# The second MLP layer of a fused attention and mixer kernel in two groups of 1024 rows instead of four of 512

## The chip, the cores and the metric

The kernel runs on one core of a Trainium2 chip. Its engines work beside each other, each through a list of instructions in a fixed order: TensorE (PE, matmuls; PEld its weight loads), VectorE (DVE), ScalarE (ACT), GpSimd (POOL) and SyncE (SP, which here only issues DMAs). They wait for each other through semaphores. The metric is the device time of one execution in microseconds.

## The reference

```python
g = _sigmoid((x * gate_w).sum(-1, keepdims=True))
a = _A_ref(x, A_wqkv, A_wo)                # attention: 2048 rows, 32 heads of 16
b = _B_ref(x, B_w1, B_w2, B_w3, B_w4)
return g * a + (1 - g) * b
# _A_ref
scores = jnp.einsum("bhqd,bhkd->bhqk", q, k) * (Dh ** -0.5)
p = _softmax(scores, axis=-1)
o = jnp.einsum("bhqk,bhkd->bhqd", p, v)
# _B_ref: x is 2048 x 512, w1 and w2 512 x 512, w3 512 x 1792, w4 1792 x 512
h = _gelu(_layernorm(x, axis=-1) @ w1)
...   # four quarters of h's columns, shifted by 1, -1, 2, -2 rows, joined to hs
x1 = x + hs @ w2
h2 = _gelu(_layernorm(x1, axis=-1) @ w3) @ w4
return x1 + h2
```

Both halves take the same x, in bfloat16.

## The kernel before

Attention is cut into 32 units. A unit is one chunk c of 512 query rows with four heads (`units`, numbered 0 to 31), and has 64 blocks of 128 keys by 512 queries: 16 key tiles for each of four heads, 2048 blocks in all. TensorE computes a block's scores into a bank of PSUM. Then the exponential is taken in one of two ways:

- On ScalarE: one ACTIVATE (in `expo`, the tile `pt`) for all blocks of a step, two blocks (1024 columns) or three (1536). A step's scores lie in the tile `stage`. There are two of these, used in turn: the scores of step k are put in place after ScalarE has read step k-2 (`score_ready`).
- On VectorE and GpSimd: a "whole" block is read from PSUM (the tile `dsc`) by a TENSOR_SCALAR that turns scores into bits of an approximate exponential (`dump`). Four such blocks of a key tile fill one room of 128x4x512 int16. Three more instructions over all of the room (`shifted`, 128x2048) give further terms, the last of them on GpSimd in part. A chain thus is four blocks; its terms go to TensorE as five times four products (`produce`). A step that has one whole block beside it has two blocks for ScalarE, a step without one has three.

The rooms are seven tiles `quad`, two in `more` and, as they come free, the chunks of `xT`; they stand in the queue `room`. A new chain starts only with enough of them (`wants_whole`).

Beside the attention runs the job list `mlp()`: the first MLP layer, then the second (512 to 1792 and back to 512). For the second, the code before goes over four chunks c of 512 rows. In each, the normed rows come transposed into `xnT`; 8 of 14 column tiles of h2 are computed into the bank for general use (`ps_y`) and copied by VectorE to `g2T` (`before_gelu`). Then `gelu_all` waits until ScalarE has its turn: ACT_TABLE_LOAD for gelu, two ACTIVATEs of 128x2048 in place, two of 128x1536 straight from `stage` tiles with the 6 tiles that are left, ACT_TABLE_LOAD for exp, and a tiny ACTIVATE (`small`). No exponentials run on ScalarE in that stretch. After it `w4_tile` multiplies by w4. The same is done once for the first layer (`hT`).

At a unit's end its sums are copied from PSUM to `accsb` (L1171), a chain of DMAs brings the reciprocals of the denominators as `bcs`, GpSimd scales (`oT`, L1201), and `out_tile` (`ps_o`) projects and mixes. The last unit is cut in three ranges of rows to shorten the end (`finish_range`); there j is one of four row tiles, and j = 0 goes through ScalarE and GpSimd (L1306, L1309), the others through VectorE (L1299).

The order of all instructions is fixed when the program is written: a planner in the kernel goes step by step through estimated times of each engine and picks what to issue next. Its rules and costs are numbers in the code: `USUAL` and `RULES` (by unit) say when whole blocks are taken, among them `WIDE`, how many whole blocks a step may have, and `MAXD`, how many key tiles a unit may give to chains; others are `VLIM`, `LASTNEED`, `LOOK`, `SPARE`. `VK` says among how many key tiles chains may be chosen.

Of the kernel before, what the change touches and what calls it, by code (L numbers as in the profile page):

```python
# [32 lines left out]
def kernel(  # L33
# [21 lines left out]
    VK = 7  # L55
# [118 lines left out]
    VLIM = 2.0  # L174
    LASTNEED = 40
# [3 lines left out]
    LOOK = 0.1  # L179
    BACK = 0.6  # L180
    RUN = 1.5
    SPARE = 1
    HOLD = (0.15, 0.5)
    MARGIN = 0.3
    CREDIT = 0.5
    LATER = 0.55
    GELU, WTWO = 1.0, 1.6
# [5 lines left out]
    SLACK = 0.25  # L193
# [206 lines left out]
    def norm_T(n, c, res):  # L400
        yield all_at(*[("xn", n, 4 * c + j) for j in range(4)])
        xnT = xtpool.tile([P, KT, CH], BF16, tag="xnT", name="xnT")
# [59 lines left out]
    def w4_tile(g2T, w4, c, t):  # L462
        yield all_at("w4", ("g", c))
        ps = gen("ps_4")
        j = t % 4
        for m in range(FT):
            bmm(ps[:], lhsT=g2T[:, m, j * P:(j + 1) * P], rhs=w4[:, m, :],
                start=(m == 0), stop=(m == FT - 1))
            if m < FT - 1:
                yield MM  # L470

        def fn(end):
            nc.vector.tensor_tensor(out=x_sb[t][:], in0=x_sb[t][:], in1=ps[:], op=ALU.add)
            at["mix", t] = end

        evac(0.69, fn)
        yield MM

    def mlp():
# [28 lines left out]
        for c in range(NC_):  # L508
            if c < NC_ - 1:
                norm(1, c + 1)  # L510
            g2T = pools["g"].tile([P, FT, CH], BF16, tag="g", name="g2T")
            for m in range(APART):
                yield from before_gelu(w3, m, res[0], g2T[:, m, :], ("z", c, m), all_at(("xnT", 1, c, KT - 1)))
            yield from gelu_all(("g", c), [g2T[:, m:m + 4, :] for m in range(0, APART, 4)],
                                all_at(*[("z", c, m) for m in range(APART)]), w3, res[0],
                                [(range(m, m + 3), g2T[:, m:m + 3, :]) for m in range(APART, FT, 3)])
            if c < NC_ - 1:
                res = []
                yield from norm_T(1, c + 1, res)
            for t in range(4 * c, 4 * c + 4):  # L520
                yield from w4_tile(g2T, w4, c, t)
# [508 lines left out]
    def exp_option():  # L1030
# [6 lines left out]
        if k in turn:  # L1037
            return turn[k][2]() if turn[k][1] else t
# [9 lines left out]
    def expo_gelu(start, k):  # L1048
        key, parts, _, _, _, ms, dst, ending = turn[k]
        if parts:  # L1050
            start += LOAD
        for part in parts:
            nc.scalar.activation(out=part, in_=part, func=ACT.Gelu_apprx_tanh)  # L1053
            start += 0.1 + part.free_size() / 1200
# [4 lines left out]
        if ending:  # L1059
            at[key] = done_exp[k]  # L1060
            nc.scalar.activation(out=small[:], in_=mhalf[:, 0:1], func=ACT.Exp)
# [176 lines left out]
    def finish_range(r, ready):  # L1238
# [41 lines left out]
        def scale(end):  # L1280
# [3 lines left out]
            for j in range(a, b):  # L1284
# [3 lines left out]
                queue["pe"].append((2 - 3 * r, 2 * MM, lambda begin, j=j: out(j), fits))  # L1288
# [238 lines left out]
```

## Time and profile before

| | |
|---|---|
| median of 3 runs | 776.76 us (775.57 to 777.45) |
| the profiled execution: its own time | 777.28 us |
| its span, first to last instruction | 775.5 us |
| mean granted TensorE clock | 0.996 of full speed |
| busy: PE, DVE, ACT, POOL | 749.0, 718.0, 757.7, 254.3 us |
| chain that ended last | ACT 51%, PE 29%, issue 16%, DVE 2% |

A row of the view of groups gives line, engine, operation, tiles and shapes, the number of instructions, then their busy time together in us and the mean duration of one in ns, then the engine's idle time before them and who ended it. Consecutive ACTIVATEs overlap in the record, so that the mean duration is more than the time from one start to the next. In the timeline a row has start, length, engine, line, operation and the number of merged instructions (the form shown is that of the first), and in brackets the idle time before it.

### The profile page before, as it was taken

How to read it: one execution, taken by the hardware profiler on the slowest of the kernel's cores; microseconds unless marked ns; L12 is line 12 of the kernel's file. 1: busy time of each engine (PE TensorE's matmuls, PEld its weight loads, DVE VectorE, ACT ScalarE, POOL GpSimd, SP SyncE). 2: the span in 40 equal slices, each digit the busy share in tenths (PEclk: the TensorE clock that was granted, in tenths of full speed). 3: DMA queues.
4: the chain of work that ended last, by engine and by line, in shares of the span. 5: the costliest groups of instructions: out<-in, count | busy, mean ns of one | idle time of the engine just before them, and what ended most of it. 6: DMA issues, size and time to landing. Idle time of an engine off the chain costs nothing.

```text
span 775.5 us, 24000 instructions
## 1 busy us (share of the span) xinstructions
PE 749.0 (97%) x10166; PEld 245.6 (32%) x10166; DVE 718.0 (93%) x1234; ACT 757.7 (98%) x731; POOL 254.3 (33%) x190
## 2 busy tenths in 40 slices
PE   8999999999999999899999999999999999999997
PEld 4334323333333232232223223322332232332233
DVE  5798999999999999899999999999999989999993
ACT  6999999999999999899999999999999999999995
POOL 3221433442313414234442333123323412443420
PEclk9999999999999999999999999999999999999999
DMA  8600012111130005002000013000040000000010
GB/s 209 192 20 17 13 50 64 31 34 42 19 36 19 19 15 127 20 16 47 20 12 27 19 33 44 18 8 19 19 53 21 16 21 25 21 23 19 20 40 28
DMA packets 52307, 29.05 MB, mean 37 GB/s; under 512 B 36712, under 2 KB 47720, under 8 KB 52200
## 3 DMA queue, kind: packets, MB, share of 16 engines
q1 hardware_dynamic: 51240, 27.00, 15.1%
q8 instruction: 79, 1.29, 0.7%
q10 hardware_dynamic: 960, 0.52, 0.2%
q14 instruction: 28, 0.23, 0.1%
HBM read 17.17 MB, written 2.35 MB: 25 GB/s over the span
## 4 chain that ended last, share of the span: by engine, by line
ACT 51%; PE 29%; issue 16%; DVE 2%; DMA 1%; POOL 0%; POOLq 0%; ACTq 0%; DVEq 0%; SPq 0%
ACT pt L1076 47%; PE acc L1089 11%; PE stage L754 9%; PE ps L271 4%; PE ps_y L271 2%; ACT g2T L1053 1%; PE ps_o L271 1%; ACT g2T L1056 1%; ACT hT L1053 1%; DMA bcs<-rec_d 1%; ACT L1053 1%; PE warm L1330 0%; DVE quad L959 0%; DMA rec_d<-rec 0%; DVE quad L1000 0%
## 5 line engine op out<-in xcount | busy, mean ns | idle before, releaser
L1076 ACT ACTIVATE pt<-stage 128x1024 bf16<-128x1024 f32 (+1 forms) x687 | 707.7, 1207 | 4.1 <-PE stage L754 2.6
L754 PE MATMUL stage<-qT,kT 32*128 32x512 bf16 (+1 forms) x1597 | 271.7, 380 | 16.7 <-ACT pt L1076 12.4
L959 DVE TENSOR_SCALAR quad<-dsc 128x512 int16<-128x512 f32 x342 | 227.6, 683 | 13.2 <-PE dsc L754 10.9
L998 POOL TENSOR_SCALAR quad<-quad 128x2048 int16<-128x2048 int16 x71 | 134.9, 1901 | 261.9 <-DVE quad L1000 145.9
L754 PE MATMUL dsc<-qT,kT 32*128 32x512 bf16 x475 | 182.6, 384 | 0.0
L754 PEld LDWEIGHTS <-kT 32*128 32x128 bf16 x2072 | 81.9, 91 | 284.0 <-issue 250.3
L1000 DVE TENSOR_SCALAR quad<-quad 128x2048 int16<-128x2048 int16 x212 | 146.8, 705 | 2.3 <-PE acc L1089 1.9
L1089 PE MATMUL acc<-pt,vp 128*17 128x512 bf16 (+2 forms) x1572 | 147.4, 379 | 1.4 <-DVE accsb L1171 0.7
L1089 PE MATMUL acc<-quad,vp 128*17 128x512 bf16 x1696 | 145.4, 382 | 0.0
L1089 PEld LDWEIGHTS <-vp 128*17 128x17 bf16 (+1 forms) x4072 | 82.7, 89 | 131.1 <-issue 95.5
L271 PE MATMUL ps<-w,g2T 128*32 128x512 bf16 x896 | 70.5, 382 | 0.0
L1201 POOL TENSOR_TENSOR oT<-accsb,bcs 128x512 bf16<-128x512 f32 x29 | 37.1, 1278 | 66.1 <-DVE quad L1000 48.8
L271 PE MATMUL ps_y<-xnT,w 128*32 128x512 bf16 x704 | 56.2, 387 | 1.0 <-DVE accsb L1171 0.8
L959 DVE TENSOR_SCALAR more<-dsc 128x512 int16<-128x512 f32 x77 | 51.2, 681 | 1.8 <-PE dsc L754 1.6
L998 POOL TENSOR_SCALAR more<-more 128x2048 int16<-128x2048 int16 x17 | 32.3, 1900 | 61.2 <-DVE more L1000 31.6
L998 POOL TENSOR_SCALAR xT<-xT 128x2048 int16<-128x2048 int16 x13 | 25.0, 1924 | 69.8 <-DVE quad L1000 31.0
L1089 PE MATMUL acc<-more,vp 128*17 128x512 bf16 x424 | 40.4, 380 | 0.0
L959 DVE TENSOR_SCALAR xT<-dsc 128x512 int16<-128x512 f32 x56 | 37.3, 681 | 2.6 <-PE dsc L754 2.2
L271 PEld LDWEIGHTS <-w 128*32 128x32 bf16 x1152 | 28.0, 96 | 34.3 <-issue 17.2
L1089 PE MATMUL acc<-xT,vp 128*17 128x512 bf16 x380 | 36.0, 383 | 0.0
L271 PE MATMUL acc<-wq,zero 128*32 128x512 bf16 x324 | 29.8, 383 | 0.0
L271 PEld LDWEIGHTS <-g2T 128*32 128x32 bf16 x896 | 19.3, 95 | 22.1 <-issue 14.3
(117 smaller groups left out, 598.4 us busy)
## 6 DMA issues: line engine op xcount, KB each, us to landing
bcs<-rec_d SPq DMA_DIRECT2D x31, 256.0 KB
w<-in_B_w_dram SPq DMA_DIRECT2D x2, 1792.0 KB
out_dram<-ot SPq DMA_DIRECT2D x15, 128.0 KB
x_sb<-in_A_x_dram SPq DMA_DIRECT2D x14, 128.0 KB
oT<-oT SPq DMA_DIRECT2D x112, 16.0 KB
w<-in_B_w_dram SPq DMA_DIRECT2D x2, 512.0 KB
wkv<-in_A_wqkv_dram SPq DMA_DIRECT2D x1, 512.0 KB
wo_all<-in_A_wo_dram SPq DMA_DIRECT2D x8, 64.0 KB
```

The source lines that it names most:

```text
L271: nc.tensor.matmul(out[j:j + 32, :], lhsT=lhsT[:, j:j + 32], rhs=rhs, tile_position=(0, j), **kwargs)
L754: nc.tensor.matmul(out, lhsT=kT[G][32 * j:32 * j + 32, cc, o:o + P], rhs=qTs[(c, G)][32 * j:32 * j + 32, a, lo:hi], start=True, stop=True, ...
L959: nc.vector.tensor_scalar(out=bits[:, r:r + wide, :], in0=dsc.rearrange("p (a c) -> p a c", c=CH), scalar1=SHIFT, scalar2=LOWEST, op0=ALU. ...
L998: behind(nc.gpsimd.tensor_scalar(out=tiles[to], in0=tiles[base], scalar1=1.0, scalar2=shift, op0=ALU.mult, op1=ALU.add))
L1000: fast["ins"] = nc.vector.tensor_scalar(out=tiles[to], in0=tiles[base], scalar1=shift, scalar2=None, op0=ALU.add)
L1053: nc.scalar.activation(out=part, in_=part, func=ACT.Gelu_apprx_tanh)
L1056: nc.scalar.activation(out=dst, in_=stages.pop(k)[:, 0:len(ms) * CH].rearrange("p (a c) -> p a c", c=CH), func=ACT.Gelu_apprx_tanh)
L1076: nc.scalar.activation(out=pt[:, 0:w], in_=stages.pop(k)[:, 0:w], func=ACT.Exp, scale=LN2 / 128.0)
L1089: nc.tensor.matmul(accs[n][32 * j:32 * j + M, lo:hi], lhsT=lhsT, rhs=p, start=(kt == 0), stop=(kt == NT - 1), skip_group_check=True, tile_ ...
L1201: behind(nc.gpsimd.tensor_tensor(out=oT, in0=tiles["accsb"][:], in1=tiles["bcs"][:], op=ALU.mult))
```

## The change

The second MLP layer takes the chunks in pairs. For the first chunk of a pair all is as before up to the gelu. Then three rooms are taken from the exponentials' queue (`lend`, each as soon as at least `KEEP` = 4 stand in it): one receives the normed, transposed rows of the second chunk, two its first 8 column tiles. Two further rooms are taken for the 6 column tiles that come straight from `stage`. One gelu stretch then serves both chunks (`gelu_both`). The room of the rows goes back after it, the other four after the second chunk's products with w4.

```diff
-    VK = 7
+    VK = 5
...
-    RULES = {... 9: {"DLIM": 1.2, "CHAINS": 2, "MANY": 2, "NEED": 26, "AHEAD": 4, "PTS": 4, "WIDE": 1, "HURRY": 4}, ...}
+    RULES = {... 9: {"DLIM": 1.2, "CHAINS": 2, "MANY": 6, "NEED": 26, "AHEAD": 20, "PTS": 6, "WIDE": 2, "MAXD": 20}, ...}
...
-    VLIM = 2.0
-    LASTNEED = 40
+    VLIM = 6.0
+    LASTNEED = 32
...
-    LOOK = 0.1
+    LOOK = 0.3
+    KEEP = 4
...
-    SPARE = 1
+    SPARE = 3
...
+    def gelu_both(c, parts, ready, direct):
+
+        yield ready
+        split = {0: parts[0:2], 1: parts[2:3], 2: parts[3:4]}
+        for i, (rhs, ms, dst) in enumerate(direct):
+            gelus.append((("g", c), split[0] if i == 0 else [], ready, w3, rhs, ms, dst, i == len(direct) - 1, split.get(i, []) if i else []))
+        yield lambda: None if gelus else 0.0
+
+    def lend():
+
+        yield lambda: max(state["t"], freed.get(id(room[0]), 0.0)) if len(room) >= KEEP else None
+        lent.append(room.popleft())
...
-        for c in range(NC_):
-            if c < NC_ - 1:
-                norm(1, c + 1)
+        for c in range(0, NC_, 2):
+            norm(1, c + 1)
             g2T = pools["g"].tile([P, FT, CH], BF16, tag="g", name="g2T")
             for m in range(APART):
                 yield from before_gelu(w3, m, res[0], g2T[:, m, :], ("z", c, m), all_at(("xnT", 1, c, KT - 1)))
...
+            for _ in range(3):
+                yield from lend()
+            other = []
+            yield from norm_T(1, c + 1, other, lent[0].bitcast(BF16))
...
+            low = [x.bitcast(BF16) for x in lent[1:3]]
+            for m in range(APART):
+                yield from before_gelu(w3, m, other[0], low[m // 4][:, m % 4, :], ("z", c + 1, m), all_at(("xnT", 1, c + 1, KT - 1)))
+            for _ in range(2):
+                yield from lend()
+            high = [x.bitcast(BF16)[:, 0:3, :] for x in lent[3:5]]
+            yield from gelu_both(c, [g2T[:, 0:4, :], g2T[:, 4:8, :]] + low, ...)
+            room.append(lent[0])
...
-        for part in parts:
+        for part in parts + later:
             nc.scalar.activation(out=part, in_=part, func=ACT.Gelu_apprx_tanh)
...
-                queue["pe"].append((2 - 3 * r, 2 * MM, lambda begin, j=j: out(j), fits))
+                queue["pe"].append((2 - 3 * r if j else -10, 2 * MM, lambda begin, j=j: out(j), fits))
```

All of the table by unit has other numbers; units 9 and 11 now allow two whole blocks in a step (`WIDE` 2). Counted over the whole program, the change gives these instructions:

| engine, instruction | before | after |
|---|---|---|
| ACT exponentials of 1024 / 1536 / 512 columns | 511 / 175 / 1 | 470 / 206 / 14 |
| ACT_TABLE_LOAD; `small` | 11; 5 | 7; 3 |
| ACT gelu of the second layer, 2048 / 1536 columns | 8 / 8 | 8 / 8 |
| DVE whole blocks read, 512 / 1024 / 1536 columns at once | 478 / 5 / 4 | 435 / 16 / 3 |
| 128x2048 terms of chains, DVE / POOL | 395 / 105 | 385 / 91 |
| PE products of chains; of exponentials from ACT, 512 columns | 2500; 1536 | 2380; 1560 |
| PE products with `zero` that keep it busy | 332 | 356 |

On ACT the first gelu stretch of the second layer looks so before (`pt` are exponentials, `g2T` the activated columns):

```order
L1076 ACTIVATE pt<-stage 128x1536 x2
L1076 ACTIVATE pt<-stage 128x1024 x2
L1053 ACT_TABLE_LOAD
L1053 ACTIVATE g2T<-g2T 128x2048 x2
L1056 ACTIVATE g2T<-stage 128x1536 x2
L1061 ACT_TABLE_LOAD
L1061 ACTIVATE small<-mhalf 128x1
L1076 ACTIVATE pt<-stage 128x1024 x9
```

After the change, the same place on ACT, where `more` and `quad` are lent rooms:

```order
L1115 ACTIVATE pt<-stage 128x1024 x6
L1090 ACT_TABLE_LOAD
L1090 ACTIVATE g2T<-g2T 128x2048 x2
L1093 ACTIVATE g2T<-stage 128x1536
L1090 ACTIVATE more<-more 128x2048
L1093 ACTIVATE g2T<-stage 128x1536
L1090 ACTIVATE quad_266<-quad_266 128x2048
L1093 ACTIVATE quad_262<-stage 128x1536
L1093 ACTIVATE quad_263<-stage 128x1536
L1100 ACT_TABLE_LOAD
L1100 ACTIVATE small<-mhalf 128x1
L1115 ACTIVATE pt<-stage 128x1536
```

Two stretches have become one, with the steps in place and those from `stage` taking turns.

On ACT behind the first layer's gelu (units 9 to 12), before:

```order
L1061 ACTIVATE small<-mhalf 128x1
L1076 ACTIVATE pt<-stage 128x1536 x4
L1076 ACTIVATE pt<-stage 128x1024 x4
L1076 ACTIVATE pt<-stage 128x1536 x5
L1076 ACTIVATE pt<-stage 128x1024 x4
```

And after, a part of the same stretch:

```order
L1115 ACTIVATE pt<-stage 128x1536 x5
L1115 ACTIVATE pt<-stage 128x512 x2
L1115 ACTIVATE pt<-stage 128x1536
L1115 ACTIVATE pt<-stage 128x512 x2
L1115 ACTIVATE pt<-stage 128x1536 x2
L1115 ACTIVATE pt<-stage 128x512 x2
L1115 ACTIVATE pt<-stage 128x1536 x3
```

Where before a chain's four blocks lie beside four steps of two blocks, here they lie beside two steps of one block each.

On PE at the very end (`end<-identf,rec` spreads reciprocals, `end<-wo_pad` is the last projection, two for a row tile), before:

```order
L1263 MATMUL end<-pick,accsb 128x4
L1275 MATMUL end<-identf,rec 32x128 x8
L1294 LDWEIGHTS oT_256
L1294 MATMUL end<-wo_pad,oT_256 128x512
L1294 LDWEIGHTS oT_257
L1294 MATMUL end<-wo_pad,oT_257 128x512
```

And after:

```order
L1302 MATMUL end<-pick,accsb 128x4
L1314 MATMUL end<-identf,rec 32x128 x4
L1333 LDWEIGHTS oT_256
L1333 MATMUL end<-wo_pad,oT_256 128x512
L1333 LDWEIGHTS oT_257
L1333 MATMUL end<-wo_pad,oT_257 128x512
L1314 MATMUL end<-identf,rec 32x128 x4
```

The projection of row tile j = 0, last of the four before, now stands first and ahead of the last range's reciprocals.

More of the change, by code (lines that the diff above doesn't have):

```diff
@@ L167 @@
+    MM = 0.212
+    TURN = 0.102
     NARROW = ("full", "attend")
@@ L192 @@
     DFILL = 1
-    SLACK = 0.25
+    SLACK = 0.3
     GAP = 0.3
@@ L398, in norm, with norm_T @@
             aside(0.41, normed(t), all_at(("rstd", n, c), "xnfree"), True)
-    def norm_T(n, c, res):
+    def norm_T(n, c, res, where=None):
         yield all_at(*[("xn", n, 4 * c + j) for j in range(4)])
-        xnT = xtpool.tile([P, KT, CH], BF16, tag="xnT", name="xnT")
+        xnT = xtpool.tile([P, KT, CH], BF16, tag="xnT", name="xnT") if where is None else where
         for j in range(4):
```

54 lines of the change are left out of this document (33 added, 21 removed).

## The prediction

> **What bounds the kernel now.** I read the page's busy times first, then the groups of ScalarE with shapes apart, then windows, and last the timeline at the places that the change touches.
>
> ```profile
> PE 749.0 (97%) x10166; PEld 245.6 (32%) x10166; DVE 718.0 (93%) x1234; ACT 757.7 (98%) x731; POOL 254.3 (33%) x190
> ...
> L1076 ACT ACTIVATE pt<-stage 128x1024 bf16<-128x1024 f32 (+1 forms) x687 | 707.7, 1207 | 4.1 <-PE stage L754 2.6
> L754 PE MATMUL stage<-qT,kT 32*128 32x512 bf16 (+1 forms) x1597 | 271.7, 380 | 16.7 <-ACT pt L1076 12.4
> ```
>
> ScalarE is busy 757.7 of 775.5 us, and in all of its 687 exponential steps it waited 4.1 us. TensorE is nearly as full, but its largest wait, 12.4 us, is for ScalarE to free a `stage`. Windows say where the rest is:
>
> ```profile
> 100.00:200.00 100.00, 96.21 (x1224) 30.30 (x1220) 97.33 (x164) 99.77 (x101) 40.61 (x25) 1.00 0.18 42
> 200.00:300.00 100.00, 96.21 (x1286) 32.28 (x1282) 98.03 (x174) 99.94 (x93) 28.82 (x20) 1.00 0.24 45
> 300.00:400.00 100.00, 96.46 (x1289) 30.57 (x1286) 92.59 (x157) 97.84 (x95) 37.81 (x24) 0.98 0.09 22
> ```
>
> The fourth busy column is ScalarE: over 99.7 of 100 us, but for one stretch with 97.84, where the granted clock is 0.98 as well. So the time is the sum of ScalarE's steps, plus that one disturbance, plus a head and an end. I cost the change on ScalarE; what falls off the other engines buys nothing unless ScalarE waits for it.
>
> **1. The exponentials on ScalarE.** These are its groups:
>
> ```profile
> L1076 ACT ACTIVATE pt<-stage 128x1024 bf16<-128x1024 f32 x511 | 482.7, 1101 | 2.3 <-PE stage L754 0.9 <-PE dsc L754 0.7
> L1076 ACT ACTIVATE pt<-stage 128x1536 bf16<-128x1536 f32 x175 | 245.9, 1521 | 1.7 <-PE stage L754 1.7
> ...
> L1053 ACT ACT_TABLE_LOAD x5 | 6.4, 1283 | 0.1
> L1061 ACT ACT_TABLE_LOAD x5 | 6.4, 1283 | 0.1
> ...
> L1076 ACT ACTIVATE pt<-stage 128x512 bf16<-128x512 f32 x1 | 0.7, 728 | 0.0
> ```
>
> Busy time over count is what a step takes of the engine: 482.7/511 = 0.945 us for two blocks, 245.9/175 = 1.405 us for three. The order after has 119 chains for 125 (2380 products of chains, 20 in a chain, for 2500), so 24 blocks more lie on ScalarE: 470 steps of two, 206 of three, 14 of one, against 511, 175 and 1. That is -41 x 0.945 = -38.7 and +31 x 1.405 = +43.6, and 13 more steps of one block.
>
> What a step of one block costs is the open price. The low end is the difference of the two rows, 1.405 - 0.945 = 0.46 us, as if nothing waited. The high end is the only such step of before:
>
> ```profile
> 756.97 2.06 ACT L1076 ACTIVATE pt<-stage 128x1536 bf16<-128x1536 f32 x2
> ...
> 758.59 1.08 PE L754 MATMUL stage<-qT,kT 32*128 32x512 bf16 x4
> ...
> 759.28 1.02 ACT L1076 ACTIVATE pt<-stage 128x1024 bf16<-128x1024 f32 x1 [0.24 <-PE stage L754]
> ```
>
> A step of three ended at 758.54 by its own length, the step of one block (728 ns long) at 756.97 + 2.06 = 759.03, so it began at 758.30. TensorE began the scores of the step after it at 758.59, when the step of three had been read, and ScalarE got them at 759.28, having stood idle 0.24. From one start to the next: 0.98 us. A step of 0.46 is too short to hide the 0.69 us from score to exponential. After the change, 12 of the 14 come in pairs, two chains' halves in a row; the second of a pair has its scores asked for earlier, and waits less unless VectorE is late with the two blocks that it reads beside it:
>
> ```profile
> L959 DVE TENSOR_SCALAR quad<-dsc 128x512 int16<-128x512 f32 x342 | 227.6, 683 | 13.2 <-PE dsc L754 10.9
> ...
> L959 DVE TENSOR_SCALAR quad<-stage 128x1024 int16<-128x1024 f32 x3 | 3.6, 1211 | 0.0
> ```
>
> Those take 1.21 us, within the 1.405 of the step of three ahead of the pair but not within 0.46. I take 0.75, between the ends: 13 x 0.75 = +9.8. Sum for the exponentials: **+14.6** (10.9 to 17.6).
>
> **2. The gelu stretches.** One of the four, on ScalarE:
>
> ```profile
> 467.13 1.28 ACT L1053 ACT_TABLE_LOAD   x1
> 468.42 3.71 ACT L1053 ACTIVATE g2T<-g2T 128x2048 bf16<-128x2048 bf16 x2
> 472.04 2.77 ACT L1056 ACTIVATE g2T<-stage 128x1536 bf16<-128x1536 f32 x2
> 474.83 1.28 ACT L1061 ACT_TABLE_LOAD   x1
> 476.12 0.20 ACT L1061 ACTIVATE small<-mhalf 128x1 f32<-128x1 f32 x1
> 476.23 6.49 ACT L1076 ACTIVATE pt<-stage 128x1024 bf16<-128x1024 f32 x7
> ```
>
> From 467.13 to 476.23 it is 9.10 us; the work in it, 468.42 to 474.83, is 6.41 and stays. The two loads and the tiny step, 2.69 us, go twice: -5.4, at most -5.7 if the overlap of a step with the next that a load breaks is counted. A load here costs its own 1.283 us and 0.01 to the next start, and it starts 0.03 or less after the step ahead. The Trainium skill, "ScalarE: Activation LUTs", section "What ACT_TABLE_LOAD costs", adds a drain of some 1.38 us to the load, about 2.66 us for a switch to another set. By that page the four switches fewer would bring an estimated 10.6 in place of 5.4, and the sum below would be 5 us lower; the trace does not agree, since the load is followed at once by the next step.
>
> In the merged stretch TensorE makes four `stage` tiles of 12 groups of strips each. Its pitch:
>
> ```profile
> 757.13 0.39 PE L271 MATMUL ps_o<-wo_all,oT 128*32 128x512 bf16 x4
> ...
> 757.77 0.62 PE L271 MATMUL ps_o<-wo_all,oT 128*32 128x512 bf16 x8
> ```
>
> Two groups of four took 0.62, one 0.39, so 0.23 a group and 2.8 us for a tile. Between two tiles ScalarE has a step in place and one from `stage`, (3.62 + 2.79)/2 = 3.2 us: covered, with 0.4 to spare, less than the 0.69 from score to step. The last tile is the one that may come late. I add +0.5 (0 to 2.0). Sum: **-4.9** (-5.7 to -3.4).
>
> **3. The end.** Row tile j = 0 is the last of four there:
>
> ```profile
> 767.65 0.39 DVE L1282 TENSOR_TENSOR oT<-accsb,end 128x256 bf16<-128x256 f32 x1
> ...
> 768.51 0.43 PE L1275 MATMUL end<-identf,rec 128*32 128x128 f32 x8 [0.30 <-DVE rec L1268]
> 768.87 1.90 PE L1294 MATMUL end<-wo_pad,oT 128*128 128x512 bf16 x8
> 769.51 2.07 DVE L1299 SCALAR_TENSOR_TENSOR ot<-end,g_fin,parts 128x512 bf16<-128x512 f32 x3
> 770.76 0.69 ACT L1306 ACTIVATE ot<-end,g_fin 128x512 f32<-128x512 f32 x1 [3.36 <-PE end L1294]
> 771.53 1.26 POOL L1309 TENSOR_TENSOR ot<-ot,parts 128x512 bf16<-128x512 f32 x1 [24.42 <-ACT ot L1306]
> 772.82 0.33 SPq L1310 DMA_DIRECT2D out_dram<-ot  x1
> ```
>
> Its rows of `oT` are there at 768.04. Projected first, in the 0.30 us hole at 768.21, it reaches ScalarE some 1.8 us earlier. It pushes the last range's reciprocals back by some 0.2, so VectorE's three tiles end at 771.58 + 0.2 = 771.8, and the last DMA is theirs: 771.8 for 772.82, **-1.0** (-1.9, if that delay is hidden, to +0.5, if a late chain holds up the last range).
>
> **4. The disturbance.** This is the stretch at 97.84:
>
> ```profile
> 320.09 1.27 POOL L1201 TENSOR_TENSOR oT<-accsb,bcs 128x512 bf16<-128x512 f32 x1 [11.17 <-DMA bcs<-rec_d]
> ...
> 321.39 0.69 DVE L1171 COPY accsb<-acc 128x512 f32<-128x512 f32 x1 [1.46 <-POOL oT L1201]
> ...
> 322.13 1.41 PE L271 MATMUL ps_y<-xnT,w 128*32 128x512 bf16 x12 [0.85 <-DVE accsb L1171]
> ...
> 325.04 1.45 ACT L1076 ACTIVATE pt<-stage 128x1536 bf16<-128x1536 f32 x1 [1.51 <-PE stage L754]
> ```
>
> The single `accsb` was free only when GpSimd had its `bcs`; the copy waited, TensorE stood still 0.85 us behind it, then ran at half pace (three groups in 1.41: 0.51 a group), and ScalarE lost 1.51 us. An order written anew may miss such a place or have others. The change adds a cause: w4's products of a pair's first chunk now come after both chunks' gelu, `out_tile` waits for them, and until it ran its rooms for `oT` are taken; the scaling waits for a room, the copy of `accsb` for the scaling, and TensorE is in order behind it. Half of it: **-1.0** (-2.0 to +2.5).
>
> **5. The rest.** VectorE reads 43 single blocks fewer (43 x 0.683 = 29 us) and 11 doubles more (13 us); TensorE has 96 products fewer in groups of four (24 x 0.23 = 5.5 us). Both are off the path. Better fed, ScalarE waits less, and steps of three leave more cover: **-1.0**. At most it could be (0.945 - 0.91) x 511 = 18 us, 0.91 being the pitch of the seven steps from 476.23 ((6.49 - 1.02)/6); I bound it at -4, and at +2 if the new order is less tight. Waits of `lend` hold up the job list alone, and the eight transposes into lent rooms replace eight others on SP: nothing, while ScalarE waits for no DMA in any row above; if that cover fails it is term 4.
>
> **Sum.** 14.6 - 4.9 - 1.0 - 1.0 - 1.0 = +6.7 us. The profiled execution took 777.28, so 784.0; it stands 0.5 above the median of the runs, so 783.5.
>
> **The rivals.**
> - *Faster: the new order feeds ScalarE without a gap.* Place: the small waits of 0.035 us in each step, 18 us in all. For: VectorE and TensorE have more air. Against: 470 steps of two remain, with the same 0.69 us from score to step. It decides once it gets back 8.3 us (6.7 and the 1.6 us of 0.2%); with half of the 18 in place of my 1.0 the sum is -1.3, and with steps of one block at 0.46 it is -5.1: 772.
> - *No change: steps of one block cost 0.46 and the disturbance is gone* (-3.8 and -1.0): +1.9, some 778.5, within 0.2% with any small help. For: the planner has put them behind long steps. Against: the row at 759.28.
> - *No change by the load's drain.* If a switch stopped ScalarE for the length of one more step that the records do not show (1.28 a load, four loads), the sum would be +1.6: 778.4. Against: 468.42 follows 467.13 + 1.28. The page named above is the reason to list it; 3 in 100.
> - *Much slower: TensorE falls to half clock in the merged stretches.* They last 2 x 6.41 + 2.69 = 15.5 us and give TensorE 48 groups x 0.23 = 11 us of its own. If it stands still at one place in each as at 321.4, ScalarE loses 2.5 us twice: 788.5. For: the 0.51 pace after 322.13. Against: 24 more products with `zero`, planned for such holes. The Trainium skill, "TensorE: Matmul & The Clock Gate", section "Why this matters for your kernels", lets an idle gap of about 3 us halve the clock; at 321.4 a visible hole of 0.85 us was followed by it, so a hole shorter than that is a risk here.
>
> **The numbers.** Forecast, slower by 778.5 to 788: 68 in 100. Half clock, over 788: 14. No change: 11 (the drain's 3 among them). Faster: 7. This measurement can tell about 0.2% (1.6 us) from no change. So faster 0.07, same 0.11, slower 0.82. The range leaves out most of the faster case, a part of no change and the far part of half clock: 777 to 790, with nearly 2 in 10 outside.
>
> **What would show it.** Groups of ScalarE: 470, 206 and 14 steps, busy time up by about 6 us; idle time ended by PE's `stage` up from 3 to some 6 us. Gelu stretches: two of about 15.5 us without idle time. The end: GpSimd's last addition before VectorE's last tile. Windows: no 100 us with ScalarE under 99. I am wrong if exponential steps of two blocks take clearly less than 0.945, or if ScalarE's busy time does not grow.

## The result and the profile after

| | before | after |
|---|---|---|
| median | 776.16 us (775.09 to 777.45, 4 runs) | 783.55 us (783.13 to 783.81, 4 runs) |
| span of the profiled execution | 775.5 us | 781.4 us |

The ratio is 1.0096, 95% interval 1.0083 to 1.0108: the change makes the kernel slower by 1%. The profiled execution of before was 1.1 us longer than the median of its runs and that of after 0.4 us shorter than its own, so the spans differ by 5.9 us where the medians differ by 7.4. Of the page after, the first part and the row of the exponentials:

```profile
PE 748.3 (96%) x10094; PEld 247.9 (32%) x10094; DVE 701.3 (90%) x1191; ACT 764.0 (98%) x728; POOL 229.0 (29%) x176
...
L1115 ACT ACTIVATE pt<-stage 128x1024 bf16<-128x1024 f32 (+2 forms) x690 | 719.6, 1206 | 4.5 <-PE stage L791 1.9
```

ScalarE has 6.3 us more work (757.7 before) and waits hardly more (4.5 us for 4.1). VectorE has 16.7 us less: there are six chains fewer, and a chain has four of the 128x2048 terms (500 for 125 chains, 476 for 119), not three. By shapes, on ScalarE:

```profile
L1115 ACT ACTIVATE pt<-stage 128x1024 bf16<-128x1024 f32 x470 | 446.1, 1089 | 1.9 <-PE stage L791 0.5 <-PE dsc L791 0.3 <-PE acc L1128 0.3
L1115 ACT ACTIVATE pt<-stage 128x1536 bf16<-128x1536 f32 x206 | 288.9, 1511 | 2.0 <-PE stage L791 1.4
L1115 ACT ACTIVATE pt<-stage 128x512 bf16<-128x512 f32 x14 | 8.7, 629 | 0.6 <-PE dsc L791 0.6
```

Counted from each start to the next, the account of ScalarE for the two profiled executions is this:

| us | before | after | difference |
|---|---|---|---|
| up to the first exponential | 8.7 | 8.4 | -0.3 |
| steps of two blocks | 474.5 (0.929 each) | 437.3 (0.930) | -37.2 |
| steps of three blocks | 236.3 (1.350) | 276.8 (1.344) | +40.6 |
| steps of one block | 1.0 (0.973) | 10.2 (0.728) | +9.2 |
| gelu stretches of the second layer | 4 x 9.10 | 15.38 + 15.54 | -5.5 |
| last exponential's start to the end | 10.4 | 9.7 | -0.7 |

The differences are taken before rounding. Their sum is +6.1; the spans differ by 5.9. One merged stretch in the timeline:

```profile
399.72 1.28 ACT L1090 ACT_TABLE_LOAD   x1
401.01 3.71 ACT L1090 ACTIVATE g2T<-g2T 128x2048 bf16<-128x2048 bf16 x2
404.63 1.43 ACT L1093 ACTIVATE g2T<-stage 128x1536 bf16<-128x1536 f32 x1
405.96 1.90 ACT L1090 ACTIVATE more<-more 128x2048 bf16<-128x2048 bf16 x1
407.76 1.44 ACT L1093 ACTIVATE g2T<-stage 128x1536 bf16<-128x1536 f32 x1
409.09 1.91 ACT L1090 ACTIVATE quad<-quad 128x2048 bf16<-128x2048 bf16 x1
410.89 2.79 ACT L1093 ACTIVATE quad<-stage 128x1536 bf16<-128x1536 f32 x2
413.69 1.28 ACT L1100 ACT_TABLE_LOAD   x1
414.99 0.20 ACT L1100 ACTIVATE small<-mhalf 128x1 f32<-128x1 f32 x1
415.10 3.69 ACT L1115 ACTIVATE pt<-stage 128x1536 bf16<-128x1536 f32 x3
```

No step waits in it. What VectorE does meanwhile shows in the windows of the same stretches, after (two) and before (four). A row has the window and its length, then the busy time and number of instructions of PE, PEld, DVE, ACT and POOL, then the granted clock; the third busy column is VectorE:

```profile
399.70:415.10 15.40, 14.90 (x257) 7.48 (x256) 4.95 (x7) 15.34 (x13) 1.28 (x1) 1.00 0.31 56
609.40:625.00 15.60, 15.25 (x263) 6.85 (x264) 9.43 (x16) 15.50 (x13) 1.29 (x1) 1.00 0.07 22
```

```profile
342.70:351.80 9.10, 9.04 (x154) 4.25 (x154) 7.70 (x12) 9.04 (x8) 2.20 (x2) 1.00 0.08 27
467.10:476.20 9.10, 9.10 (x162) 4.36 (x157) 8.28 (x11) 9.04 (x8) 3.37 (x2) 1.00 0.52 34
565.90:575.00 9.10, 9.00 (x161) 3.87 (x152) 8.87 (x14) 9.05 (x7) 1.90 (x1) 1.00 0.42 67
671.60:680.70 9.10, 8.92 (x159) 3.82 (x154) 7.76 (x12) 9.04 (x8) 1.90 (x1) 1.00 0.04 10
```

Before, it was busy in 32.6 of 36.4 us of gelu; after, in 14.4 of 31.0. The timeline of VectorE in the first stretch tells what it waits for:

```profile
400.91 0.68 DVE L1037 TENSOR_SCALAR quad<-xT 128x2048 int16<-128x2048 int16 x1
405.38 0.69 DVE L1037 TENSOR_SCALAR xT<-xT 128x2048 int16<-128x2048 int16 x1 [3.79 <-PE acc L1128]
405.99 0.69 DVE L1037 TENSOR_SCALAR more<-more 128x2048 int16<-128x2048 int16 x1
412.83 1.76 DVE L996 TENSOR_SCALAR quad<-stage 128x1536 int16<-128x1536 f32 x1 [6.15 <-PE stage L791]
```

It waits 3.79 us for TensorE's products of a chain that is under way, then 6.15 us for the first whole blocks behind the stretch. While both `stage` tiles serve the gelu there are no whole blocks to read. Chains that are under way keep VectorE going through a stretch of 9 us, but not through one of 15.

### The profile page after: what moved, and what is told of

It is laid out like the page before. It is cut to its first block, busy times and chain, and to the rows that moved or that the text cites. A ratio compares the mean times of both kernels' runs of the same rounds, so it can differ in the third digit from the quotient of the medians.

```text
span 781.4 us, 23791 instructions
## 1 busy us (share of the span) xinstructions
PE 748.3 (96%) x10094; PEld 247.9 (32%) x10094; DVE 701.3 (90%) x1191; ACT 764.0 (98%) x728; POOL 229.0 (29%) x176
## 3 DMA queue, kind: packets, MB, share of 16 engines
q8 instruction: 79, 1.29, 0.7%
## 4 chain that ended last, share of the span: by engine, by line
ACT 41%; PE 34%; DVE 12%; issue 12%; POOL 1%; DVEq 0%; ACTq 0%; POOLq 0%
ACT pt L1115 38%; PE acc L1128 12%; PE stage L791 10%; DVE quad L996 4%; PE ps L272 3%; PE ps_y L272 2%; DVE quad L1037 2%; PE ps_v L272 1%; PE stage L272 1%; DVE st L370 1%; PE ps_k L272 1%; PE ps_q L272 1%; DVE more L1037 1%; ACT hT L1090 1%; PE ps_o L272 1%
## 5 line engine op out<-in xcount | busy, mean ns | idle before, releaser
L1115 ACT ACTIVATE pt<-stage 128x1024 bf16<-128x1024 f32 (+2 forms) x690 | 719.6, 1206 | 4.5 <-PE stage L791 1.9
L996 DVE TENSOR_SCALAR quad<-dsc 128x512 int16<-128x512 f32 x313 | 211.7, 697 | 14.9 <-PE dsc L791 13.3
L791 PE MATMUL dsc<-qT,kT 32*128 32x512 bf16 x461 | 171.8, 384 | 0.0
L1037 DVE TENSOR_SCALAR quad<-quad 128x2048 int16<-128x2048 int16 x225 | 156.3, 712 | 4.4 <-PE acc L1128 4.4
L996 DVE TENSOR_SCALAR more<-dsc 128x512 int16<-128x512 f32 (+1 forms) x74 | 52.8, 728 | 5.2 <-PE dsc L791 4.7
L1035 POOL TENSOR_SCALAR more<-more 128x2048 int16<-128x2048 int16 x13 | 24.7, 1897 | 74.5 <-DVE quad L1037 30.6
L272 PEld LDWEIGHTS <-w 128*32 128x32 bf16 x1152 | 28.4, 96 | 32.6 <-issue 13.9
L272 PE MATMUL ps_y<-xnT,w 128*32 128x512 bf16 x448 | 34.9, 382 | 0.4 <-DVE g2T L415 0.4
L272 PE MATMUL ps<-w,g2T 128*32 128x512 bf16 x448 | 34.6, 383 | 0.1
L1128 PE MATMUL acc<-xT,vp 128*17 128x512 bf16 x284 | 27.8, 381 | 0.0
L1210 DVE COPY accsb<-acc 128x512 f32<-128x512 f32 x31 | 21.2, 683 | 4.1 <-POOL oT L1240 2.4
```

The costliest lines, as they stand in the source:

```text
L272: nc.tensor.matmul(out[j:j + 32, :], lhsT=lhsT[:, j:j + 32], rhs=rhs, tile_position=(0, j), **kwargs)
L791: nc.tensor.matmul(out, lhsT=kT[G][32 * j:32 * j + 32, cc, o:o + P], rhs=qTs[(c, G)][32 * j:32 * j + 32, a, lo:hi], start=True, stop=True, ...
L996: nc.vector.tensor_scalar(out=bits[:, r:r + wide, :], in0=dsc.rearrange("p (a c) -> p a c", c=CH), scalar1=SHIFT, scalar2=LOWEST, op0=ALU. ...
L1035: behind(nc.gpsimd.tensor_scalar(out=tiles[to], in0=tiles[base], scalar1=1.0, scalar2=shift, op0=ALU.mult, op1=ALU.add))
L1037: fast["ins"] = nc.vector.tensor_scalar(out=tiles[to], in0=tiles[base], scalar1=shift, scalar2=None, op0=ALU.add)
L1115: nc.scalar.activation(out=pt[:, 0:w], in_=stages.pop(k)[:, 0:w], func=ACT.Exp, scale=LN2 / 128.0)
```

## The experiments

Three theories stood against each other on why 24 blocks came to ScalarE and where 7 us went. A: the lent rooms cost the chains, and the time follows ScalarE's sum. B: the planner's new numbers make the loss, above all the steps of one block. C: the long stretches starve the other engines.

**Two rooms fewer, nothing else.** The code before with

```diff
-    room = deque(epool.tile([P, 4, CH], I16, name=f"quad{i}")[:] for i in range(7))
+    room = deque(epool.tile([P, 4, CH], I16, name=f"quad{i}")[:] for i in range(5))
```

> The code before with five tiles quad in place of seven, so two rooms fewer for chains all the time; four gelu stretches, numbers of the planner and the end as before. Its order has 119 chains and 1572 blocks on ScalarE (496 steps of two, 193 of three, one of one), as many blocks as after the change. Theory A (rooms: fewer rooms give fewer chains, and ScalarE pays for each block): by the pitches of the trace of before, 0.929 us for a step of two and 1.350 for a step of three, 722.3 us of exponentials for 711.8, so +10.5: some 786.7. Theory B (the new numbers of the planner, with steps of one block, make the loss): none of them is here, 776 to 778. Theory C (the long merged gelu stretches starve the other engines): none here, 776 to 778.

Measured: 813.71 us, ratio 1.0487 (1.0471 to 1.0503). The direction is A's, the size nobody's. At their shortest pitches (0.904 for two blocks, 1.331 for three, the commonest values; some 0.48 for one, an estimate by their difference) its steps need 705.7 us for 695.3, +10.4, as expected; but they took 748.5 for 711.8. That is 42.8 us over the shortest sum, where before has 16.4. ScalarE's list of waits names the cause of most of the 26 us between (us in all, times, longest):

```profile
ACT pt L1076 <- PE acc L1089: 21.7, 17, 6.8
```

A `pt` tile is written again only when its products are made. At a unit's end these stand in TensorE's order behind the last terms of a chain; where a chain is late, the six `pt` tiles fill up and ScalarE stops. The longest of these waits ended so:

```profile
144.54 0.39 PE L1089 MATMUL acc<-quad,vp 128*17 128x512 bf16 x4
144.75 0.40 PE L1089 MATMUL acc<-pt,vp 128*32 128x512 bf16 x4
...
145.25 1.94 ACT L1076 ACTIVATE pt<-stage 128x1024 bf16<-128x1024 f32 x2 [6.81 <-PE acc L1089]
```

That the planner's numbers do not fit five rooms is the likely reason, but no run shows it. So an order that is planned anew measures its own waits as well as the edit; from here on that is theory D.

**Two more switches.** The code before with, ahead of the `small` step behind each stretch of the second layer,

```diff
+            if key != "h":
+                nc.scalar.activation(out=small[:], in_=mhalf[:, 0:1], func=ACT.Exp)
+                nc.scalar.activation(out=small[:], in_=mhalf[:, 0:1], func=ACT.Gelu_apprx_tanh)
             nc.scalar.activation(out=small[:], in_=mhalf[:, 0:1], func=ACT.Exp)
```

> The code before with, behind each of the four gelu stretches of the second layer, a tiny Exp and a tiny Gelu ahead of the tiny Exp that is there: eight more table loads and eight more tiny steps, and otherwise the same order. It leaves nothing out. Theory A (a load costs ScalarE its own 1.29 us from start to start, a tiny step 0.11): 8 x 1.40 = +11.2, some 787.4. Rival (a load also drains for as long again, as the 2.66 us of the Trainium skill's page ScalarE: Activation LUTs, section What ACT_TABLE_LOAD costs, would have it): +22, some 798. Rival (the stretches are not on the path): no change, 776.

Measured: 795.99 us, ratio 1.026 (1.0246 to 1.0274), +20.0: near the drain's figure, but not by its mechanism. The timeline of ScalarE behind the first stretch:

```profile
348.60 1.28 ACT L1062 ACT_TABLE_LOAD   x1
349.89 0.20 ACT L1062 ACTIVATE small<-mhalf 128x1 f32<-128x1 f32 x1
350.11 1.28 ACT L1063 ACT_TABLE_LOAD   x1
351.40 0.20 ACT L1063 ACTIVATE small<-mhalf 128x1 f32<-128x1 f32 x1
351.62 1.28 ACT L1064 ACT_TABLE_LOAD   x1
...
353.03 2.83 ACT L1079 ACTIVATE pt<-stage 128x1024 bf16<-128x1024 f32 x3
356.68 1.02 ACT L1079 ACTIVATE pt<-stage 128x1024 bf16<-128x1024 f32 x1 [0.81 <-PE dsc L754]
```

From load to load it is 1.51 us, with no drain: 1.29 for the load and 0.22 for the tiny step. A stretch is 12.14 us for 9.10, four of them +12.2. The other 7 us are in the exponentials. TensorE stood idle for 2.60 us there, and the granted clock fell to half:

```profile
354.08 0.61 PE L754 MATMUL stage<-qT,kT 32*128 32x512 bf16 x2 [2.60 <-ACT pt L1079]
```

```profile
340.00:353.00 13.00, 10.91 (x175) 4.94 (x175) 10.61 (x16) 12.88 (x12) 4.37 (x4) 0.99 0.14 37
353.00:360.00 7.00, 5.92 (x48) 1.06 (x47) 3.11 (x6) 5.22 (x7) 1.48 (x2) 0.53 0.44 65
```

The granted clock in the second window is 0.53. Behind the other three stretches TensorE's hole was 3.24, 2.85 and 3.23 us, and half clock lasted 6.8, 3.4 and 6.8 us. Exponentials took 718.6 us for 711.8, +6.8: step by step against the same order in before, 8.5 us more behind the four stretches, and 2.1 less at 322, where the disturbance did not occur in this execution. This is the rival of half clock in the flesh; the change avoids it, with 14.90 of 15.40 us busy on TensorE and a clock of 1.00 in its merged stretches.

**The pairs with the old numbers.** The code after with the table and costs of before:

```diff
-    RULES = {... 9: {"DLIM": 1.2, "CHAINS": 2, "MANY": 6, "NEED": 26, "AHEAD": 20, "PTS": 6, "WIDE": 2, "MAXD": 20}, ...}
+    RULES = {... 9: {"DLIM": 1.2, "CHAINS": 2, "MANY": 2, "NEED": 26, "AHEAD": 4, "PTS": 4, "WIDE": 1, "HURRY": 4}, ...}
...
```

> The code after with all numbers of the planner as before (USUAL, RULES and the costs; KEEP stays 4; VK 5 or 7 gives the same order counts). Its order has 119 chains as well: 502 steps of two, 189 of three, one of one, and no steps of one block in pairs. Theory A (rooms): exponentials 502 x 0.929 + 189 x 1.350 + 1.0 = 722.5 for 711.8, +10.7; gelu stretches -5.5; the end -0.6: +4.6, some 780.8. Theory B (the new numbers make the loss): the pairs alone gain, 776.2 - 5.5 - 0.6 = some 770. Theory C (long stretches starve engines): as after the change, 783.5 or over.

Measured: 798.61 us, ratio 1.0295 (1.0281 to 1.0309). Theory B falls: without the new numbers it is slower still, with as many blocks on ScalarE (1572). Their shortest sum is 705.8 us; they took 740.2. One line of waits holds half of the 34 us between, and nearly all that is over the 16.4 of before:

```profile
ACT pt L1115 <- PE acc L1128: 17.6, 5, 9.8
```

So the new numbers are worth 15 us to this structure (798.61 against 783.55), and leave it 1% short.

**The end alone.** The code before with the last changed line alone (`2 - 3 * r if j else -10`).

> The code before with only the last changed line: row tile j = 0 is projected first at the end. All theories: from the last exponential to the end of the span 8.88 us before and 8.23 after the change, so -0.65, some 775.5; the prediction's term was -1.0 (-1.9 to +0.5). If the end of before was set by another tile, no change.

Measured: 774.79 us against 775.98, ratio 0.9984 (0.9975 to 0.9993): faster than both kernels, the only one here, if by 0.2% only. From the start of the last exponential to the end it took 9.45 us for 10.38. Up to the last unit this is the order of before, and yet the disturbance at 322 is not there:

```profile
300.00:400.00 100.00, 97.01 (x1316) 31.26 (x1312) 94.52 (x159) 99.61 (x96) 38.62 (x25) 1.00 0.09 22
```

```profile
321.02 0.83 PE L271 MATMUL ps_y<-xnT,w 128*32 128x512 bf16 x12 [0.15 <-DVE accsb L1171]
```

TensorE waited 0.15 us for the copy of `accsb`, 0.85 in the profiled execution of before, and the exponentials there took 2.0 us less.

**The old end in the code after.** The reverse edit.

> The code after without its last changed line: j = 0 is projected last at the end again. All theories: the counterpart of the end alone, which gained 1.2 us on the code before (ratio 0.9984): +0.6 to +1.2 over after, some 784.4.

Measured: 785.17 us, ratio 1.0112 (1.0097 to 1.0127) to before. By the medians the line is worth 1.2 us in before and 1.6 here, a little over what was expected; from the last exponential's start to the end it is 0.9 in both (9.71 us for 10.60 here). The end after, in its timeline:

```profile
774.92 0.61 PE L1333 MATMUL end<-wo_pad,oT 128*128 128x512 bf16 x2
...
775.63 0.69 ACT L1345 ACTIVATE ot<-end,g_fin 128x512 f32<-128x512 f32 x1 [1.44 <-PE end L1333]
...
776.40 1.26 POOL L1348 TENSOR_TENSOR ot<-ot,parts 128x512 bf16<-128x512 f32 x1 [7.89 <-ACT ot L1345]
776.46 2.07 DVE L1338 SCALAR_TENSOR_TENSOR ot<-end,g_fin,parts 128x512 bf16<-128x512 f32 x3 [0.15 <-PE end L1333]
...
778.12 0.90 SPq L1340 DMA_DIRECT2D out_dram<-ot  x2
```

GpSimd is done at 777.66, VectorE at 778.53: the last DMA is VectorE's now.

**Pairs without lent rooms.** The code after with the second chunk written over the first:

```diff
-            yield from norm_T(1, c + 1, other, lent[0].bitcast(BF16))
+            yield from norm_T(1, c + 1, other, res[0])
...
-            low = [x.bitcast(BF16) for x in lent[1:3]]
+            low = [g2T[:, 0:4, :], g2T[:, 4:8, :]]
...
-            high = [x.bitcast(BF16)[:, 0:3, :] for x in lent[3:5]]
+            high = [g2T[:, APART:APART + 3, :], g2T[:, APART + 3:FT, :]]
```

> The code after, but the second chunk of a pair takes no rooms: its rows and its 14 column tiles are written over those of the first chunk (xnT, g2T), so that the second layer is computed from overwritten tiles for the first chunk; instructions, sizes and the planner's numbers are those of after. All rooms stay with the exponentials. Its order has 1572 blocks on ScalarE again (473 steps of two, 204 of three, 14 of one). Theory A (the lent rooms cost the chains): with these numbers the order does not use the rooms, so the count says 0.1 us of ScalarE more than after; but VectorE should be full in the merged stretches and behind them, where it was busy 4.95 of 15.4 us after the change. Theory C (the merged stretch itself leaves VectorE without whole blocks, since both stage tiles serve the gelu): VectorE stays under 10 of 15.4 us there, and the time is that of after, 782 to 786.

Measured: 790.7 us, ratio 1.0185 (1.017 to 1.02). The windows of its merged stretches:

```profile
393.40:408.70 15.30, 14.86 (x265) 7.61 (x261) 7.65 (x9) 15.26 (x11) 1.69 (x1) 1.00 0.18 39
615.70:631.10 15.40, 15.40 (x274) 7.30 (x267) 7.30 (x12) 15.34 (x12) 1.28 (x1) 1.00 0.11 32
```

VectorE is busy in 15.0 of 30.7 us with all rooms at hand, 14.4 of 31.0 with five lent: the hole belongs to the merged stretch, as C has it. The time is over what C expected. The last ACTIVATE waited for TensorE, so that the end took 13.8 us for 9.7, and the exponentials took 727.6 us for 724.3:

```profile
784.25 0.69 ACT L1334 ACTIVATE ot<-end,g_fin 128x512 f32<-128x512 f32 x1 [6.45 <-PE end L1322]
```

A new order's own waits, as in theory D, would explain both; no run shows it.

**The same with the old numbers.** Both edits together.

> As the run of pairs without lent rooms, with the planner's numbers of before. 1560 blocks on ScalarE (516 steps of two, 176 of three): 12 fewer than the pairs with lent rooms under the same numbers, 12 more than before. Theory A: rooms are half of the 24 blocks, so by the pitches 516 x 0.929 + 176 x 1.350 = 717.0 of exponentials for 711.8, gelu -5.5, end -0.6: -0.9, some 775, if nothing waits. Theory D (an order not made for its structure waits at the ends of units, as the pairs with old numbers did, 17.6 us of ScalarE behind PE's acc): 785 to 805, with that wait in ScalarE's list.

Measured: 809.07 us, ratio 1.0425 (1.0409 to 1.044), theory D's case: ScalarE waited 24.9 us for PE's `acc` and 10.2 at the end. Only its count of blocks says something of the rooms: under the old numbers four groups leave ScalarE 1548 blocks, pairs without lending 1560, pairs with lending 1572.

**One whole block a step.** The code after with `"WIDE": 1` in units 9 and 11.

> The code after with WIDE 1 in units 9 and 11, as everywhere else: no steps of one block, 497 of two, 194 of three, 1576 blocks. Theory B (the pairs of one-block steps are what costs): by the pitches 497 x 0.930 + 194 x 1.344 = 722.9 for 724.3 after, so -1.4 at most, some 782. Theory D (an order changed in one number waits elsewhere): over 783.5, with ScalarE waiting for PE's acc.

Measured: 806.87 us, ratio 1.0398 (1.0379 to 1.0417). The steps of one block cannot be told from the order that goes with them: without them it waits 9.5 us for PE's `acc` and 11.7 at the end.

**More work for ScalarE in the same order.** The code before; k counts the steps.

```diff
...
-        nc.scalar.activation(out=pt[:, 0:w], in_=stages.pop(k)[:, 0:w], func=ACT.Exp, scale=LN2 / 128.0)
+        for _ in range(2 if k > EARLY + 20 and w == 2 * CH and k % 40 < 2 and again.append(k) is None and len(again) <= 12 else 1):
+            nc.scalar.activation(out=pt[:, 0:w], in_=stages[k][:, 0:w], func=ACT.Exp, scale=LN2 / 128.0)
+        stages.pop(k)
```

> The code before with 12 exponential steps of two blocks, spread over the units, done twice in a row (same tile in, same tile out), all else in the same order: 24 blocks more for ScalarE and nothing else. Theory A (the time follows the sum of ScalarE's steps): 12 x 0.904 to 0.945 us = +10.8 to +11.3, some 787. Rival (ScalarE has slack that the records call busy): under +5, below 781.

Measured: 790.34 us, ratio 1.0208 (1.0164 to 1.0252), so +12.7 to +19.5 us, over theory A's figure. The rival falls. In the profiled execution the span grows by 12.2 us and the exponentials by 12.1 (723.9 for 711.8); 12 steps at the shortest pitch are 10.8. Ahead of the end the granted clock fell to half twice in it, once in before:

```profile
219.95:223.40 3.45, 3.45 (x31) 0.78 (x34) 2.65 (x5) 2.84 (x3) 0.00 (x0) 0.51 0.82 92
404.30:407.70 3.40, 3.27 (x26) 0.76 (x25) 1.89 (x3) 2.88 (x4) 0.00 (x0) 0.50 0.06 15
```

ScalarE has no slack: 24 blocks cost all of their length and some more.

**More work for VectorE in the same order.** The code before; at every seventh chain,

```diff
...
-                fast["ins"] = nc.vector.tensor_scalar(out=tiles[to], in0=tiles[base], scalar1=shift, scalar2=None, op0=ALU.add)
+                for _ in range(2 if i == 1 and len(again) % 7 == 3 else 1):
+                    fast["ins"] = nc.vector.tensor_scalar(out=tiles[to], in0=tiles[base], scalar1=shift, scalar2=None, op0=ALU.add)
```

> The code before with 18 of the 128x2048 terms on VectorE done twice in a row (same in, same out), all else in the same order: 18 x 0.61 us, from start to start, = 11 us more for VectorE. Theory A (ScalarE alone sets the time; VectorE's 16.7 us less after the change bought nothing): 0 to +3, 776 to 779. Rival (VectorE, busy 96 to 98 of 100 us, binds as much): +8 to +11, 784 to 787.

Measured: 782.77 us, ratio 1.0086 (1.0071 to 1.0101), +7.0 for 11 us of work, between the two. In the profiled execution the exponentials took 716.5 us for 711.8, although the disturbance did not occur (1.8 us less there). ScalarE waits through `dsc`, whose bank comes free when VectorE has read it, 3.7 us in all for 0.7:

```profile
L1079 ACT ACTIVATE pt<-stage 128x1024 bf16<-128x1024 f32 x511 | 483.5, 1082 | 6.1 <-PE dsc L754 3.7 <-PE stage L754 0.9 <-PE acc L1092 0.5
```

## Why the prediction was right, point by point

The forecast was 783.5 us, the median is 783.55. The mechanism held: ScalarE's steps set the time, and 24 blocks more cost it more than the merged stretches save. That the figures agree within 0.1 us is luck. The sum was +6.7; the profiled executions differ by 5.9 and the medians by 7.4. And inside the sum two errors cancel:

- **Exponentials, with disturbance and rest: +14.6 - 1.0 - 1.0 = +12.6.** Measured +12.6, but by other parts. "Busy time over count is what a step takes" is a misreading: where shapes change, the overlap of two steps is counted in both groups (482.7 + 245.9 + 0.7 = 729.3 us by shapes, 707.7 for all steps together). From start to start the steps of before took 0.929 and 1.350 us, not 0.945 and 1.405. So the new counts of steps of two and three cost +3.8, not +4.9, and with +9.2 for the steps of one block that is +13.0, not +14.6. Disturbance and rest, here the change in the pitches of steps of two and three, came to -0.4, not -2.0.
- **A step of one block: 0.75 us.** Measured 0.728. Three of the six firsts of a pair took 0.76 to 0.84, one 0.88, two 0.56 to 0.59; the seconds 0.49 to 0.96, hardly shorter in the mean (0.70 for 0.73). So "the second of a pair waits less" was not borne out; the price between the ends was. Four of the seconds started 0.06 to 0.24 us late behind `dsc`, VectorE's bank, which the prediction had as its exception. Where ScalarE waited for `stage` behind such steps (five places, 220.6 to 294.6), it began 0.50 us after the first score, not 0.69.
- **Gelu stretches: -4.9.** Measured -5.5. The 0.5 that I added for TensorE being late was 0.16, in the second stretch alone. The loads cost what their rows said, and two more switches confirm 1.29 us from a load to the next step. The drain that the Trainium skill, "ScalarE: Activation LUTs", section "What ACT_TABLE_LOAD costs", adds to a load does not show in any of these runs.
- **The end: -1.0.** Measured -0.7 in the spans, and -0.9 in the profiled executions with that line alone put in or out. The order of events is the one described.
- **The disturbance: half of it.** It is gone; no clock under 1.00 shows in after. But the new order need not be the reason: the profiled executions of the end alone, of two more switches and of more work for VectorE had the order of before at this place and no disturbance, 1.8 to 2.1 us less. So it comes in some executions of one order and not in others. The cause that the change was to add, late products with w4, does not show: at the copies of `accsb` VectorE waited 2.4 us for GpSimd in all, 3.1 before.
- **Half clock in the merged stretches** did not come about. Why the rival was real shows the run with two more switches: a hole of 2.60 us in TensorE, and 0.53 of the clock. The Trainium skill, "TensorE: Matmul & The Clock Gate", section "Why this matters for your kernels", warns of idle gaps of over about 3 us; here 2.60 us was enough, and before the change, at 322.1, less. The merged stretches have no such hole. The pace of 0.51 us a group at 322.13 was read too long: a group alone took 0.61 there (at 324.87), so it is (1.41 - 0.61)/2 = 0.40.
- **What was too strong:** that VectorE is "off the path". What fell off it bought nothing that shows: with 16.7 us less, the pitches of steps of two and three are within 0.006 us of before. But eleven more microseconds on VectorE cost seven. It is not the first bound, but in a fixed order it is the next one at many places.
- **Two signs failed.** I expected idle time ended by `stage` to double, and it fell from 2.6 to 1.9: the 1.51 us of the disturbance are gone from it, and the steps of one block brought only 1.0, since their other waits stand at `dsc` (0.6) and as lost overlap. And I expected no window under 99, where the 100 us with the steps of one block have 98.04:

```profile
200.00:300.00 100.00, 94.54 (x1274) 31.17 (x1271) 96.50 (x153) 98.04 (x95) 33.67 (x20) 1.00 0.15 34
```

Where the expected gain went: the merge does save its 5.5 us. But the order after has six chains fewer, and their 24 blocks come back to ScalarE as 12.6 us. At the shortest pitches its steps need 705.8 us for 695.3, the same as in the other orders with 1572 blocks, so some 10.4 of the 12.6 are the blocks themselves. The other 2 are longer waits: the 14 steps of one block, 0.728 for some 0.48, have 3.5 us of them, and the other steps have less than before.

Why there are fewer chains is shown in part. VectorE loses 12.8 us of work in the stretches (31.0 - 14.4 less 36.4 - 32.6), and that the stretch itself makes this hole is shown, by the pairs without lent rooms. That the hole leads to fewer chains is argued. How many of the 24 blocks are due to the hole and how many to the lent rooms is open: under the old numbers the counts go 12 and 12, under the new ones the count is 1572 with and without lending, and no run had the rooms free with an order that did not wait elsewhere.

## What to carry to other kernels

Where two engines share one kind of work, a fixed cost saved on the bounding one (here 2.7 us for a pair of table loads) must be set against the work that the other no longer takes over. So count the instructions of the bounding engine in the new order first, at their pitch from start to start; busy time by shapes over count is more than the pitch where steps overlap. A long stretch in which the bounding engine changes its task can also starve an engine that lives on its buffers. When a planner writes the order, an edit and an untuned order are measured together: compare the sum of the steps at their shortest pitch with the sum as it ran, and look at who ended the waits in between.

## What the runs showed of the hardware

Two table loads and a tiny step cost 2.69 us on ScalarE, each load 1.29 us to the next start in all 19 places but the first (run with two more switches). Besides, the step ahead of a load loses its overlap with the next: in the first merged stretch the last gelu step took 1.47 us from its start to the load, the one ahead of it 1.33 to the next step.

The half clock did not need one long hole. In before, TensorE was busy for half of the 3.4 us ahead of it, with holes of 0.85 us at most:

```profile
318.80:322.20 3.40, 1.69 (x22) 0.75 (x25) 1.94 (x4) 3.40 (x4) 1.27 (x1) 1.00 0.02 7
322.25:325.66 3.41, 3.41 (x31) 0.94 (x28) 3.41 (x6) 1.90 (x2) 0.00 (x0) 0.50 0.12 26
```

In the run with two more switches it was busy for 1.72, 1.13, 0.55 and 0.99 us of the 3.4 us ahead of the four falls. In the end alone, where the same place kept its full clock, it was 2.30 of 3.40 us (317.8 to 321.2), and the merged stretches, with less than 0.6 us idle in 15.4, kept it as well. What busy share is enough no run shows.
